# Cached decode attention, two blocks on one core: block B's output projection summed in four PSUM columns and stored element by element from two queues, instead of transposed to rows first

## The chip, the core and the metric

The kernel runs on one core of a Trainium2 chip. The metric is the device time of one execution, in microseconds (us). Before the change the median of three runs is 824.31 us (824.25 to 824.35).

## What is computed

Two independent blocks, A and B, each decode one token (one query row `x` of 512 values) with 32 heads of 128 and a cache of 16384 keys and values per head. A attends to all 16384 positions, B to the last 4096 only.

```python
q = (x @ wq).reshape(B, Sq, Hq, Dh).transpose(0, 2, 1, 3)
scores = einsum("bhqd,bhkd->bhqk", q, k) * (Dh ** -0.5)    # B: k, v = the last 4096 positions
p = softmax(scores, axis=-1)
o = einsum("bhqk,bhkd->bhqd", p, v)
y = o.transpose(0, 2, 1, 3).reshape(B, Sq, Hq * Dh) @ wo   # wo: 4096 x 512
out = concatenate([y_A, y_B], axis=-1)                     # 1 x 1 x 1024, bf16
```

The change lies in the last product, for B: 512 output values, each a sum over the 4096 rows of `wo`.

## The kernel before, in words

Keys, values and weights are bf16 and come from HBM in transfers of 2 or 4 MB (the pieces at the end are smaller), almost all issued by SyncE (SP). The work is cut into 20 units: B's first, then A's sixteen (two heads each), then B's other three. For each unit VectorE (DVE) multiplies a key tile by the broadcast query (L437) and adds up over the head's width in a tree of additions (L449, L456). ScalarE (ACT) makes the exponentials (L516), TensorE (PE) multiplies them by the values (L564). Two key tiles and one value tile are in turn refilled as they come free.

Every operation is recorded with what it reads and writes. The recorder works out the semaphore waits, and each engine's instructions run in the order in which they were recorded. A transfer is issued by the queue of the engine it was recorded on: SP's (`L.dma_start`) or ACT's (`S.dma_start`).

The end of the program, where the change lies, is in this order:

- SP issues the last half tile of B's values and then B's `wo` in five pieces of 16, 8, 4, 3 and 1 rows per partition (`wo_pieces`, L765). After these SP has nothing left but the store of B's result and the wait at the end.
- PE projects A's result as one row (`project_out_rows`, L640); ACT copies it and stores it with its own queue (L646).
- The last unit's scores, softmax and products with the values follow (L604, each half scaled by DVE at L611). `permute_o` (L620 to L632) then puts B's 4096 attention outputs into `OpB`, 128 partitions by 32.
- `project_out_columns` does B's projection. For each piece of `wo`, as it lands, PE does 4 matmuls per row of the piece (L656): a 128x128 block of `wo` is the weight, one column of `OpB` the moving side, so that 128 of the 512 outputs come as one PSUM column. Each piece has four columns of its own in the bank `OC2`, so there are 20 in all.
- DVE adds the five pieces (L665), into `cols`, 128 partitions by 4, f32. PE transposes it into 4 rows of 128 (L669). DVE casts these to bf16 (L671). SP stores the rows, 4 of 256 bytes (L672).
- SP waits for both stores (the semaphores `outA` and `outB`), and the program's closing barrier follows.

PE's program is cut at the marked operations in `parts`; the first piece's matmuls of the projection are the last mark. The cut stays at the same operation in both kernels.

Of the kernel before, what the change touches and what calls it, by code (L numbers as in the profile page):

```python
# [10 lines left out]
F32 = mybir.dt.float32  # L11
BF16 = mybir.dt.bfloat16
P = 128
ACT = mybir.ActivationFunctionType
ALU = mybir.AluOpType
AX = mybir.AxisListType

HQ, DH = 32, 128
# [209 lines left out]
def kernel(  # L228
# [19 lines left out]
    DN = A_wo.shape[1]  # L248
# [7 lines left out]
    def sb(name, shape, dtype):  # L256
        return pool.tile(shape, dtype, tag=name, name=name)

    def pst(name):
        return psum.tile([P, 512], F32, tag=name, name=name)  # L260
# [6 lines left out]
    identf = sb("identf", [P, P], F32)  # L267
# [10 lines left out]
    p_t = sb("p", [P, 2 * CH], BF16)  # L278
# [2 lines left out]
    pm_t = sb("pm", [P, 2 * CH * 4], BF16)  # L281
    r_t = sb("r", [P, 8], F32)
    osb = sb("osb", [P, 512], F32)
    cols = sb("cols", [P, 4], F32)
    sm = pst("sm")
    oc_t = pst("oc")
    TP = [pst(f"tp{i}") for i in range(2)]
    OC2 = pst("oc2")
# [16 lines left out]
    st = _Stream(tc)  # L305
    V, T_, S, G, L = nc.vector, nc.tensor, nc.scalar, nc.gpsimd, nc.sync
# [339 lines left out]
        st.op("ACT", lambda: S.dma_start(out=out[0, 0:1, 0:DN], in_=row), r=["osb"], w=["outA"], dma="outA")  # L646

    def project_out_columns(s, key, pieces):
        nf, npc = DN // P, len(pieces)
        ps = OC2[:, 0 : npc * nf].rearrange("p (k c) -> p k c", k=npc)  # L650
        r0 = 0
        for k, n in enumerate(pieces):
            def mms(k=k, n=n, r0=r0):
                for c in range(nf):
                    for r in range(r0, r0 + n):
                        x = T_.matmul(  # L656
                            ps[:, k, c : c + 1], lhsT=s.wo_t[:, r, c * P : (c + 1) * P], rhs=s.Op[:, r : r + 1],
                            start=(r == r0), stop=(r == r0 + n - 1),
                        )
                return x  # L660

            st.op("PE", mms, r=["Op" + s.n, f"{key}.{k}"], w=["oc2"])
            r0 += n
        first = st.ops["PE"][-npc]
        st.op("DVE", lambda: V.tensor_reduce(  # L665
            out=cols[:, :], in_=ps.rearrange("p k c -> p c k"), axis=AX.X, op=ALU.add
        ), r=["oc2"], w=["cols"])
        pr = TP[0][0:nf, 0:P]
        st.op("PE", lambda: T_.transpose(pr, cols[:, :], identf[:, :]), r=["cols", "identf"], w=["tp0"])  # L669
        rows = p_t[0:nf, 0:P]  # L670
        st.op("DVE", lambda: V.tensor_copy(rows, pr), r=["tp0"], w=["p.0", "p.1"])  # L671
        st.op("SP", lambda: L.dma_start(out=out[0, 0, DN : 2 * DN].rearrange("(c f) -> c f", c=nf), in_=rows),  # L672
              r=["p.0"], w=["outB"], dma="outB")
        return [first]

    wo_pieces = (16, 8, 4, 3, 1)
# [3 lines left out]
    for s in (B, A):  # L680
        s.x_row = flat(KS[1][0:1, :, :])[:, x0 : x0 + D]
        for a, b in x_pieces:
            st.op("ACT", lambda s=s, a=a, b=b: S.dma_start(out=s.x_row[:, a:b], in_=s.x[0, 0:1, a:b]),
                  w=[f"x{s.n}.{a}"], dma=f"x{s.n}{a}")
# [7 lines left out]
        out=identf[:, :], in_=identf[:, :], compare_op=ALU.not_equal, fill=1.0, base=0,  # L692
# [7 lines left out]
    for s in (B, A):  # L700
# [9 lines left out]
          w=["k10", "k11", *(f"x{n}.{a}" for n in "AB" for a, _ in x_pieces)] + [f"k10.{j}" for j in range(4)], dma="K10")  # L710

    parts = []
    for T, un in enumerate(units):
# [5 lines left out]
        if un.last:  # L719
            W, wk = KS[NT % 2], f"k{NT % 2}"  # L720
            s = A
# [41 lines left out]
    r0 = 0  # L763
    for i, n in enumerate(wo_pieces):
        st.op("SP", lambda r0=r0, n=n: L.dma_start(out=B.wo_t[:, r0 : r0 + n, :], in_=src[:, r0 : r0 + n, :]),  # L765
              r=["v1"], w=[f"wo.{i}"], dma=f"woB{i}")
# [12 lines left out]
    parts.append(st.ops["PE"][-1])  # L779
    mark = permute_o(B)  # L780
    parts += project_out_columns(B, "wo", wo_pieces)
    st.op("SP", lambda: None, r=["outA", "outB"], w=["end"])
    with tc.tile_critical(no_gpsimd_drain=True):
        st.finish(mark, parts)

# [29 lines left out]
```

## Time and profile before

| | us |
|---|---|
| median of the 3 runs | 824.31 |
| the profiled execution's own time | 824.25 |
| its span, from the first to the last instruction | 822.5 |
| DVE busy | 750.4 (91% of the span) |
| PE busy | 197.9 (24%) |
| ACT busy | 60.0 (7%) |
| last matmul of B's projection ends | 818.92 |
| SP issues the store of B's result | 819.89 |

The profiled execution's time is 1.8 us above its span: that part lies ahead of the first or behind the last instruction. The span is in microseconds from the first instruction. In the profile's lines "L656" is line 656 of the kernel, "out<-in" names the tiles written and read, "SPq" and "ACTq" are the instructions with which SP and ACT issue transfers, and a bracket at the end of a line gives the idle time ahead of it and who ended it. The core has 16 DMA engines, and a DMA packet is one run of bytes that one of them moves.

### The profile page before, as it was taken

What the parts mean: (1) busy time and instruction counts of PE and PEld (TensorE: products, weight loads), DVE (VectorE), ACT (ScalarE), POOL (GpSimd) and SP (SyncE); (2) the same over time, 40 slices, a digit from 0 to 9 for tenths busy, and PEclk for the clock granted to TensorE, in tenths of its full rate; (3) what the DMA queues carried; (4) which work ended last, traced back from release to release, by engine and by line L of the source; (5) the groups of instructions that cost most, each with busy time, mean ns of one, the idle gap of its engine ahead of it and who ended that gap; (6) DMA issues with size and microseconds to landing.
All of it is one profiled execution on the core that took longest, in us unless ns stands there. A gap on an engine that the chain in (4) does not pass through costs nothing. (4 is left out here: it accounts for less than half of the span.)

```text
span 822.5 us, 5105 instructions
## 1 busy us (share of the span) xinstructions
PE 197.9 (24%) x1985; PEld 99.0 (12%) x1985; DVE 750.4 (91%) x258; ACT 60.0 (7%) x168; POOL 0.7 (0%) x6
## 2 busy tenths in 40 slices
PE   3401212203030303030303212030303030303176
PEld 1100101101010101010101101010101010101035
DVE  2999899999999999999999999999999999999960
ACT  0101000001010100000000001010100000010111
POOL 0000000000000000000000000000000000000000
PEclk9765656565565655565655565555656555655575
DMA  9999999999999999999999999999999999999997
GB/s 383 433 433 433 457 412 450 418 447 421 444 424 441 427 437 430 437 430 437 430 437 430 437 430 437 430 437 430 437 430 437 430 422 445 422 433 431 432 432 298
DMA packets 8094, 352.44 MB, mean 429 GB/s; under 512 B 915, under 2 KB 1046, under 8 KB 1302
## 3 DMA queue, kind: packets, MB, share of 16 engines
q1 hardware_dynamic: 8072, 352.33, 99.2%
q8 instruction: 6, 0.10, 0.0%
q14 instruction: 2, 0.02, 0.0%
q10 hardware_dynamic: 14, 0.00, 0.0%
HBM read 352.32 MB, written 0.00 MB: 428 GB/s over the span
## 5 line engine op out<-in xcount | busy, mean ns | idle before, releaser
L449 DVE TENSOR_TENSOR k<-k 128x16384 bf16<-128x16384 bf16 (+3 forms) x84 | 333.3, 3968 | 2.2
L437 DVE TENSOR_TENSOR k<-k,qA 128x16384 bf16<-128x16384 bf16 x32 | 277.8, 8682 | 21.2 <-DVEq L122 21.1
L564 PE MATMUL oA<-v,pm 128*8 128x512 bf16 x1024 | 89.4, 525 | 111.0 <-PEq L122 111.0
L437 DVE TENSOR_TENSOR k<-k,qB 128x16384 bf16<-128x16384 bf16 x8 | 69.4, 8679 | 1.0 <-DVEq L122 1.0
L471 PE MATMUL sm<-identf,m 128*1 128x128 f32 x24 | 8.1, 369 | 207.8 <-PEq L122 207.8
L493 PE MATMUL sm<-one_f,Mr 1*128 1x1 f32 x48 | 12.4, 335 | 188.8 <-PEq L122 188.8
L564 PEld LDWEIGHTS oA<-v,pm 128*8 128x8 bf16 x1024 | 30.1, 110 | 163.7 <-issue 155.3
L456 DVE TENSOR_REDUCE sc<-k 128x256 f32<-128x2048 bf16 (+1 forms) x21 | 45.9, 2185 | 0.7
L493 PEld LDWEIGHTS sm<-one_f,Mr 1*128 1x128 f32 x48 | 11.2, 300 | 195.1 <-issue 195.1
L512 ACT ACTIVATE bias<-sm 128x1 f32<-128x1 f32 (+1 forms) x20 | 3.4, 171 | 412.0 <-ACTq L122 412.0
L471 PEld LDWEIGHTS sm<-identf,m 128*1 128x1 f32 x24 | 1.7, 80 | 209.7 <-issue 209.7
L576 ACT ACTIVATE osb<-oA,r 128x512 f32<-128x512 f32 x16 | 11.0, 687 | 214.1 <-ACTq L122 214.1
L564 PE MATMUL oB<-v,pm 128*16 128x512 bf16 x192 | 17.6, 546 | 23.1 <-PEq L122 23.1
L586 PE MATMUL oc<-selA,osb 128*128 128x2 f32 x128 | 16.4, 250 | 15.6 <-PEq L122 15.6
L586 PEld LDWEIGHTS oc<-selA,osb 128*128 128x128 f32 x128 | 15.5, 191 | 23.2 <-issue 23.2
L544 PE MATMUL sm<-cs,rowsA 128*128 128x1 f32 x32 | 8.9, 348 | 32.3 <-PEq L122 32.3
L502 ACT ACTIVATE pm<-p,maskA 128x256 bf16<-128x256 bf16 x32 | 14.5, 500 | 0.5
L544 PEld LDWEIGHTS sm<-cs,rowsA 128*128 128x128 f32 x32 | 8.0, 311 | 33.2 <-issue 33.2
L419 PE MATMUL tp<-v,osb 128*128 128x512 bf16 x32 | 9.1, 454 | 10.6 <-DMA v<-in_A_wq_dram 10.6
L516 ACT ACTIVATE p<-sc,bias 128x256 bf16<-128x256 f32 (+1 forms) x24 | 11.3, 470 | 0.6
L488 DVE TENSOR_REDUCE M<-sm 1x2 f32<-1x128 f32 (+1 forms) x20 | 6.0, 298 | 5.8 <-DVEq L122 5.8
L465 DVE TENSOR_REDUCE m<-sc 128x1 f32<-128x256 f32 (+1 forms) x20 | 8.4, 420 | 2.8
(73 smaller groups left out, 108.0 us busy)
## 6 DMA issues: line engine op xcount, KB each, us to landing
k<-in_B_k_cache_dram SPq DMA_DIRECT2D x8, 4096.0 KB, 35.9
v<-in_B_v_cache_dram SPq DMA_DIRECT2D x7, 4096.0 KB, 29.3
v<-in_B_wq_dram SPq DMA_DIRECT2D x1, 4096.0 KB, 12.2
v<-in_A_wq_dram SPq DMA_DIRECT2D x1, 4096.0 KB, 30.5
k<-in_A_wo_dram SPq DMA_DIRECT2D x1, 4096.0 KB, 33.5
k<-in_B_v_cache_dram SPq DMA_DIRECT2D x1, 4096.0 KB, 42.9
v<-in_B_wo_dram SPq DMA_DIRECT2D x1, 2048.0 KB, 25.1
v<-in_B_wo_dram SPq DMA_DIRECT2D x1, 1024.0 KB, 27.0
```

What stands on the lines that cost most here:

```text
L419: x = T_.matmul(out_ap, lhsT=s.xb[:, j, c, :], rhs=wq[:, c, j, g : g + 4, :], start=(k == 0), stop=(k == n - 1),)
L437: return V.tensor_tensor(out=k, in0=k, in1=s.q[:, bass.ds(i, 1), :].broadcast_to([P, CH, DH]), op=ALU.mult)
L449: st.op("DVE", lambda it=None, w=w: V.tensor_tensor(out=k[:, :, 0:w], in0=k[:, :, 0:w], in1=k[:, :, w : 2 * w], op=ALU.add), r=keys, w=keys)
L456: st.op("DVE", lambda it=None: V.tensor_reduce(out=sc[:, l0:l1], in_=un.K[:, l0:l1, 0:8], axis=AX.X, op=ALU.add), r=[f"k{un.k}{u}" for u i ...
L471: i = T_.transpose(sm[0:1, v * P : (v + 1) * P], m_t[:, v : v + 1], identf[:, :])
L493: i = T_.matmul(sm[:, 256 + v : 257 + v], lhsT=Mr[:, v * P : (v + 1) * P], rhs=one_f[:, :], start=True, stop=True,)
L502: return S.activation(out=out, in_=in_, func=ACT.Copy, scale=mask)
L516: st.op("ACT", lambda it=None, v=v: S.activation(out=p_t[:, v * n : (v + 1) * n], in_=sc[:, v * n : (v + 1) * n], func=ACT.Exp, scale=inv, ...
L544: i = T_.matmul(sm[v * w : (v + 1) * w, 264:265], lhsT=s.rows[:, :, :, :].rearrange("p r a b -> p (r a b)"), rhs=cs[:, v : v + 1], start=T ...
L564: x = T_.matmul(s.o[r0 : r0 + un.rows, :], lhsT=un.pm[:, l, :, :].rearrange("p a b -> p (a b)"), rhs=VS[:, 4 * l : 4 * l + 4, :], start=(i ...
L576: st.op("ACT", lambda it=None: S.activation(out=osb[:, :], in_=s.o[:, :], func=ACT.Copy, scale=r_t[:, 0:1]), r=["o" + s.n, "r"], w=["osb"] ...
L586: x = T_.matmul(oc_t[:, 0:w], lhsT=osb[:, j * P : (j + 1) * P], rhs=sel[:, j, :], start=(j == 0), stop=(j == 3),)
```

## The change

`project_out_columns` is rewritten. All five pieces add into the same four PSUM columns: only the first matmul of all has `start`, only the last has `stop`. DVE copies the four columns as bf16 into `cols` (now 128 x 4, bf16). The transpose on PE and the second cast on DVE are gone. The result is stored straight from `cols`. In `cols`, partition f holds outputs f, 128+f, 256+f and 384+f, so neighbours in a partition are 256 bytes apart in the output and every 2-byte element is a run of its own: 128 x 2 elements in a store by SP and 128 x 2 in one by ACT. SP's wait at the end is for three semaphores in place of two. On every other line the instructions of each engine and their order are the same in both kernels.

```diff
-    cols = sb("cols", [P, 4], F32)
+    cols = sb("cols", [P, DN // P], BF16)
...
     def project_out_columns(s, key, pieces):
-        nf, npc = DN // P, len(pieces)
-        ps = OC2[:, 0 : npc * nf].rearrange("p (k c) -> p k c", k=npc)
+        nf = DN // P
+        ps = OC2[:, 0:nf]
         r0 = 0
         for k, n in enumerate(pieces):
-            def mms(k=k, n=n, r0=r0):
+            def mms(r0=r0, n=n):
                 for c in range(nf):
                     for r in range(r0, r0 + n):
                         x = T_.matmul(
-                            ps[:, k, c : c + 1], lhsT=s.wo_t[:, r, c * P : (c + 1) * P], rhs=s.Op[:, r : r + 1],
-                            start=(r == r0), stop=(r == r0 + n - 1),
+                            ps[:, c : c + 1], lhsT=s.wo_t[:, r, c * P : (c + 1) * P], rhs=s.Op[:, r : r + 1],
+                            start=(r == 0 and c == 0), stop=(r == HQ - 1 and c == nf - 1),
                         )
                 return x
 
             st.op("PE", mms, r=["Op" + s.n, f"{key}.{k}"], w=["oc2"])
             r0 += n
-        first = st.ops["PE"][-npc]
-        st.op("DVE", lambda: V.tensor_reduce(
-            out=cols[:, :], in_=ps.rearrange("p k c -> p c k"), axis=AX.X, op=ALU.add
-        ), r=["oc2"], w=["cols"])
-        pr = TP[0][0:nf, 0:P]
-        st.op("PE", lambda: T_.transpose(pr, cols[:, :], identf[:, :]), r=["cols", "identf"], w=["tp0"])
-        rows = p_t[0:nf, 0:P]
-        st.op("DVE", lambda: V.tensor_copy(rows, pr), r=["tp0"], w=["p.0", "p.1"])
-        st.op("SP", lambda: L.dma_start(out=out[0, 0, DN : 2 * DN].rearrange("(c f) -> c f", c=nf), in_=rows),
-              r=["p.0"], w=["outB"], dma="outB")
+        first = st.ops["PE"][-len(pieces)]
+        st.op("DVE", lambda: V.tensor_copy(cols[:, :], ps), r=["oc2"], w=["cols"])
+        half = nf // 2
+        for eng, e, key, c0 in (("SP", L, "outB0", 0), ("ACT", S, "outB1", half)):
+            to = out[0, 0, DN + c0 * P : DN + (c0 + half) * P].rearrange("(c f) -> f c", c=half)
+            st.op(eng, lambda e=e, to=to, c0=c0: e.dma_start(out=to, in_=cols[:, c0 : c0 + half]),
+                  r=["cols"], w=[key], dma=key)
         return [first]
...
-    st.op("SP", lambda: None, r=["outA", "outB"], w=["end"])
+    st.op("SP", lambda: None, r=["outA", "outB0", "outB1"], w=["end"])
```

## The prediction

> **What bounds the kernel now.** I read the first page for the span, then the chain of work that ended last, in order of time, then the timeline of the last 5 us, then SP's own waits, and last the view of DMA traffic in short windows. The page says that the kernel streams its caches at one rate throughout, with VectorE nearly full beside it:
>
> ```profile
> PE 197.9 (24%) x1985; PEld 99.0 (12%) x1985; DVE 750.4 (91%) x258; ACT 60.0 (7%) x168; POOL 0.7 (0%) x6
> ...
> DMA  9999999999999999999999999999999999999997
> ```
>
> The DMA row is at nine tenths or more in 39 of 40 slices; the change touches neither the streams nor DVE's work on them. It can act only behind the last load. The chain shows where that is:
>
> ```profile
> 790.02 28.25 DMA v<-in_B_wo_dram
> ...
> 818.31 0.61 PE oc L656 x16
> ...
> 818.95 0.19 DVE cols L665
> ...
> 819.18 0.39 PE tp L669
> ...
> 819.59 0.28 DVE p L671
> ```
>
> The last piece of B's `wo` lands at 818.27, PE's last 16 matmuls end at 818.92, and then a reduction, a transpose and a cast run one after another, with nothing beside them. The timeline gives the store that follows, and SP's waits give how long SP then stands:
>
> ```profile
> 819.89 0.35 SPq L672 DMA_DIRECT2D out_dram<-p  x1
> ```
>
> ```profile
> SPq L672 <- DVE p L671: 29.0, 1, 29.0
> ...
> SPq L124 <- DMA out_dram<-p: 0.8, 1, 0.8
> ```
>
> SP waits 29.0 us for the cast, issues from 819.89 to 820.24, and waits 0.8 us for the store, until about 821.08. From there to the end of the span (822.5) is the closing barrier, 1.4 us, the same in both kernels. So what is at stake is 818.92 to 821.08, 2.16 us of 824.25: 0.97 us of work ahead of the store and 1.19 us of store. A measurement of this kernel can tell about 0.2%, 1.65 us, from no change. The program's own time, 824.25, is 0.06 below the median of the runs, 824.31; I add the sum to 824.25 and give the result for the runs, since 0.06 is smaller than any doubt below.
>
> **What is removed.** The matmuls stay: 128 at L656 in the same order and the same five pieces, writing other columns; nothing in their rows (163 to 187 ns each) hangs on the column, so 0. The reduction becomes a copy of the same PSUM bank, 128x4 bf16 from 128x4 f32. The kernel has exactly that form at its start:
>
> ```profile
> 9.81 0.16 DVE L399 CAST xTB<-tp 128x4 bf16<-128x4 f32 x1 [6.35 <-PE tp L392]
> ```
>
> So the copy begins at 818.95 and ends at 819.11. The stores can issue 0.02 later (the cast of before ended at 819.87, its store issued at 819.89), at 819.13. Against 819.89 that is **-0.76 us**, all of it on the path. It is also all that the change can win: the transpose, its two hand-overs and the cast. What is late next is the store itself.
>
> **What is added: 512 single elements.** Before, 4 runs of 256 bytes. Now 256 runs of 2 bytes on SP's queue and 256 on ACT's. The trace has no run of 2 bytes, so each stage of the store is bounded by rows.
>
> *Issue.* The rows are in the lists of the two lines that issue loads and of the one that issues `wo`:
>
> ```profile
> L335 SPq DMA_DIRECT2D v<-in_A_v_cache_dram x16: 327/328/334, 88.8 to 671.7; - x16
> ...
> L335 SPq DMA_DIRECT2D k<-in_B_k_cache_dram x8: 535/576/643, 1.4 to 718.8; - x8
> ```
>
> ```profile
> L765 SPq DMA_DIRECT2D v<-in_B_wo_dram x5: 432/432/592, 788.4 to 790.5; - x5
> ```
>
> With 128 rows an issue takes 0.33 to 0.64 us, and 0.43 for `wo`; the store of before took 0.35 with 4. I take 0.43: **+0.08** (from -0.02 to +0.29). ACT's issue runs beside SP's: ACT has been idle since 813.74 (L632), and behind the store it has only the barrier; behind SP's store is only the wait at the end. At the kernel's start ACT and SP issued at the same moment, and ACT's issue took 0.53 where its others took 0.21 to 0.38. So a collision of two issues is worth at most 0.32; I take 0.
>
> *From issue to the packets.* The store of before, in the DMA view of 820.6 to 820.8 (slices of 5 ns):
>
> ```profile
> DMA  0000000000000010112101001001000000000000
> ...
> DMA packets 8, 0.00 MB, mean 5 GB/s; under 512 B 8, under 2 KB 8, under 8 KB 8
> ...
> q1 hardware_dynamic: 8, 0.00, 3.0%
> ```
>
> Its first packet moves at 820.67, 0.43 after the issue ended, the last at 820.74. They are four runs of 256 bytes and four 4-byte semaphore writes: 3.0% of 16 engines' 0.2 us is 96 ns for 8, and in the packet records 15 ns for a run and 9 ns for a semaphore write. The only transfer with 128 rows that meets idle DMA engines is the first load: issued 0.96 to 1.38, and in the view of 1.9 to 2.7 its engines start between 2.00 and 2.66:
>
> ```profile
> DMA  0000999900999000009000000090000090900900
> ```
>
> That is 0.62 to 1.28 after the issue, +0.13 to +0.79 against the 0.49 of the old store's last packet. It reads HBM and is the kernel's first, so it is a high bound for a store; the low bound is 0. I take **+0.45**, the middle of the load's two ends.
>
> *The elements.* If they are dealt evenly, 512 over 16 engines are 32 each, and 2 semaphore writes. The nearest rows are the 15 ns of the smallest data packet written to HBM, and 9 ns, which is a 4-byte write. At 15 ns: 32 x 15 + 2 x 9 = 0.50 us, less the 0.02 that an engine had before: **+0.48** (+0.28 at 9 ns). The upper end is the time from the last packet to its landing, 820.74 to about 821.07, 0.33 us: paid by each element in turn, it is 32 x 0.33 = 10.6 us. The ends are far apart; the packet rows are nearer, since writes of before were sent within 15 ns of each other on one engine without waiting for a landing (run, then semaphore write). The landing of the last write itself, 0.33, stays.
>
> A rule bears on this size. The Trainium skill (VectorE: DVE Perf Modes, "The three transpose paths") says that a plain strided copy used as a transpose is 19 times slower than the transposing DMA, which takes 1309 ns for 128x128: as an estimate, 24.9 us for 16384 elements on 16 engines, 24 ns for one. By it the elements would add 0.77 and not 0.48, and the time would be about 824.9; no run here shows such a copy yet.
>
> *The end.* SP's wait is for one semaphore more; its branch with a wait took 33 ns (L335): **+0.03**.
>
> **The sum:** -0.76 + 0.08 + 0.45 + 0.48 + 0.03 = **+0.28**, so 824.25 + 0.28 = 824.5, and with the 0.06 to the median 824.6. With every low bound: -0.76 - 0.02 + 0 + 0.28 + 0 = -0.50, 823.8.
>
> **The rivals.**
>
> *A 2-byte write holds its engine (slower).* In place: between the first and the last packet of the two stores. All but the elements adds up to -0.20, so the change is slower by 1.65 us once the 34 packets cost 1.85 us more, about 57 ns an element. That is a sixth of the 0.33 us to a landing: it decides when an engine has fewer than six element writes on the way at once, or when writes to neighbouring addresses queue at the memory (512 elements fall into 1 KB of output). Three at once: 32 x 0.11 = 3.5, less 0.20, +3.3: 827.6. One at a time: +10.4, 834.7. [...] Against it: the 256-byte and 4-byte packets of 15 and 9 ns. Chance 0.42. The Trainium skill (DMA: Bandwidth & Descriptors, "Specifications") has a rule of this kind: a transfer below 512 bytes is read, modified and written. The 256-byte runs of before are below that too and took 15 ns, so the trace does not show it as a price per run; for 2 bytes no run does yet.
>
> *The elements are as cheap as the semaphore writes and the engines start together (a gain, but a small one).* This is the -0.50 above, 823.8. It needs 9 ns an element and a start like that of 4 runs. It is inside the same band as the forecast, and I count it there: 0.10 of the 0.55.
>
> *Faster by over 1.65 us.* The whole stretch at stake is 2.16 us, and the store alone cannot be shorter than its landing and its issue, about 1.1. Only a shift elsewhere in the program, which no edit makes, could do it: 0.03.
>
> **How the numbers follow.** Forecast, no change within 0.2%: 0.55 (its own range 823.8 to 825.9). Slower by over 0.2%: 0.42. Faster by over 0.2%: 0.03. The range 823.8 to 828.5 takes in the forecast and the rival up to about 140 ns an element; I leave out some 0.13 above and 0.04 below.
>
> **What would show each step.** In the changed profile: a DVE copy of some 0.16 us at L667 right behind the last matmul, and two issues at L671 some 0.24 us after that matmul, side by side; an issue of 0.33 to 0.64 us; some 512 more packets under 512 bytes; and SP's wait for the stores in place of 0.8 us, near 1.8. A wait of 3 us or more is the slower rival, and the DMA view then tells whether the packets themselves are long or the landing is late. If the copy or the issue is not where I put it, the gain of 0.76 is wrong; if ACT's issue starts when SP's ends, the two queues share what I took to be separate.

## The result, and the profile after

The changed kernel takes 837.24 us (median of 4 runs, 836.72 to 837.6) against 824.33 for the kernel before (4 runs, 824.25 to 824.36): a ratio of 1.0156, 95% interval 1.0139 to 1.0174. It is 12.9 us slower, and lies above the predicted range of 823.8 to 828.5.

The profiled execution took 837.60 with a span of 835.8, against 824.25 and 822.5. On its page the last of the 40 slices is almost empty; one slice is 21 us:

```profile
DMA  9999999999999999999999999999999999999991
GB/s 381 463 411 452 415 436 446 414 440 449 415 434 449 421 433 439 423 442 430 430 445 423 430 452 423 430 445 420 439 430 430 430 439 420 436 433 432 427 422 41
DMA packets 8630, 352.44 MB, mean 422 GB/s; under 512 B 1451, under 2 KB 1582, under 8 KB 1838
```

The third line shows 536 more packets under 512 bytes than the 915 before: 512 single elements and 32 semaphore writes, where the old store had 8 packets. The chain in order of time, and the end of the timeline:

```profile
818.37 0.61 PE oc L658 x16
818.98 0.02 issue
819.00 0.16 DVE cols L667
```

```profile
819.00 0.16 DVE L667 CAST cols<-oc 128x4 bf16<-128x4 f32 x1 [6.45 <-PE oc L658]
819.19 0.41 SPq L671 DMA_DIRECT2D out_dram<-cols  x1
819.20 0.47 ACTq L671 DMA_DIRECT2D out_dram<-cols  x1
```

From the last matmul's end (818.98) to the issue is 0.21 us, where it was 0.97. Then no engine has anything to do until SP's wait is over. SP's waits say for what:

```profile
SPq L671 <- DVE cols L667: 28.6, 1, 28.6
...
SPq L124 <- DMA out_dram<-cols: 14.7, 1, 14.7
```

SP waits 14.7 us for the stores in place of 0.8. The DMA view of 820 to 821 (slices of 25 ns) shows when the packets moved, and the list of L671 when the stores landed, counted from the start of their issue. A landing is the moment at which the profile records the last of the store's 16 semaphore increments:

```profile
DMA  0000056999777787952000000000000000000000
...
DMA packets 544, 0.00 MB, mean 1 GB/s; under 512 B 544, under 2 KB 544, under 8 KB 544
```

```profile
L671 SPq DMA_DIRECT2D out_dram<-cols x1: 408/408/408, 819.2 to 819.2; - x1
L671 ACTq DMA_DIRECT2D out_dram<-cols x1: 475/475/475, 819.2 to 819.2; - x1
...
DMA to landing us min/median/max: 15.1/15.2/15.3
```

All 544 packets (512 elements and 32 semaphore writes) lie in one band from 820.11 to 820.49. Then the records show no packet, and the semaphore increments come from 828.44 to 834.46. The DMA engines had let go of the last element 14 us before the store was confirmed as written.

The spans' difference is 13.34 us. From the two traces: the last matmul 0.06 later, -0.76 to the issue, +0.06 for the longer SP issue, +14.03 from the issue's end to the last landing (0.83 before, 14.86 after), -0.05 behind it. That adds up to 13.34.

### The profile page after: what moved, and what is told of

It reads as the page before. It is cut to its first block, busy times and chain, and to the rows that moved or that the text cites. A ratio compares the mean times of both kernels' runs of the same rounds, so it can differ in the third digit from the quotient of the medians.

```text
span 835.8 us, 5103 instructions
## 1 busy us (share of the span) xinstructions
PE 198.8 (24%) x1984; PEld 99.4 (12%) x1984; DVE 749.9 (90%) x257; ACT 60.0 (7%) x168; POOL 0.7 (0%) x6
## 5 line engine op out<-in xcount | busy, mean ns | idle before, releaser
L564 PE MATMUL oA<-v,pm 128*8 128x512 bf16 x1024 | 91.7, 537 | 111.1 <-PEq L122 111.1
L419 PE MATMUL tp<-v,k 128*128 128x512 bf16 x32 | 9.9, 486 | 2.5 <-DMA v<-in_B_wq_dram 2.5
```

What stands on the lines that cost most here:

```text
L419: x = T_.matmul(out_ap, lhsT=s.xb[:, j, c, :], rhs=wq[:, c, j, g : g + 4, :], start=(k == 0), stop=(k == n - 1),)
L564: x = T_.matmul(s.o[r0 : r0 + un.rows, :], lhsT=un.pm[:, l, :, :].rearrange("p a b -> p (a b)"), rhs=VS[:, 4 * l : 4 * l + 4, :], start=(i ...
```

## The experiments

Three theories of the 14 us. M: the memory takes small writes to one region in turn, whatever their address. E: each DMA engine has one small write on the way at a time. L: writes into the same 64-byte stretch of the output go one after another, different stretches beside each other. The measure is the time from the stores' first packet to their last landing, in the trace's records: 0.40 us before, 14.35 after. Runs without an interval are single looks, and the changed kernel's own four runs span 0.9 us, so differences of some tenths of a us between them say nothing. No run repeats the time from first packet to last landing. Each edit is against the changed kernel unless the text says otherwise; "..." marks lines left out.

### Half the elements

```diff
-        for eng, e, key, c0 in (("SP", L, "outB0", 0), ("ACT", S, "outB1", half)):
+        for eng, e, key, c0 in (("SP", L, "outB0", 0),):
...
-    st.op("SP", lambda: None, r=["outA", "outB0", "outB1"], w=["end"])
+    st.op("SP", lambda: None, r=["outA", "outB0"], w=["end"])
```

> The changed kernel, but ACT's store is left out (outputs 256 to 511 of B are not written): 256 single elements instead of 512. In the changed kernel the 544 packets are over 0.4 us after the first, and the last landing comes 14.35 us after the first packet. Theory M (the memory takes the 512 small writes to the same 1 KB one after another, 14.35 / 512 = 28 ns each): 256 x 28 = 7.2 us from first packet to landing, time about 830.4. Theory E (each of the 16 DMA engines has one small write on the way at a time, 14.35 / 32 = 0.45 us each): 16 each, 7.2 us as well, about 830.4. Theory L (writes into one 64-byte stretch of the output go one after another, 32 in each, 0.45 us each, different stretches beside each other): still 32 per stretch, 14.3 us, about 837.5.

Measured: 838.09 us, 14.90 from the first packet to the last landing.

```profile
SPq L124 <- DMA out_dram<-cols: 15.4, 1, 15.4
```

Half the writes, half the writes per engine and one queue in place of two, and the wait is as long. M and E fall. What stayed the same is how densely the elements lie: 32 in each 64 bytes.

### The same elements, farther apart

Both stores, 2 x 256 elements, go into a scratch tensor with a gap between neighbours; B's half of the output is not written. G is the gap in elements.

```diff
+        apart = nc.dram_tensor("apart", (DN, G), BF16, kind="Internal").ap()
...
-            to = out[0, 0, DN + c0 * P : DN + (c0 + half) * P].rearrange("(c f) -> f c", c=half)
+            to = apart[c0 * P : (c0 + half) * P, 0].rearrange("(c f) -> f c", c=half)
```

> The changed kernel with the same two stores of 256 single elements each, but into a scratch tensor in HBM where neighbours lie 64 bytes apart (32 KB in all) instead of into the output (B's half of the output is not written). Theory L: no two elements in one stretch, so landing within 1 us of the packets, about 824. Theory E: unchanged, 14.3 us, about 837.5. Theory M: between, by how large the region is whose writes queue: unchanged if 32 KB counts as one, less if it is spread over several.

> As the run with 64 bytes between neighbours, with 512 bytes (256 KB in all). Theory E: unchanged, about 837.5. Theories L and M: landing within 1 us of the packets, about 824; if M's queue is one for all small writes, unchanged.

Measured: 824.35 us at 64 bytes, 824.00 at 512.

```profile
SPq L124 <- DMA apart<-cols: 1.4, 1, 1.4
```

That is SP's wait at 64 bytes; at 512 it is 1.2. The packets are as many and as short as in the changed kernel (7 to 9 ns each), from the same queues, and the 14 us are gone. E falls a second time, and L's forecast holds. That the destination is now a scratch tensor is not the reason: with 4 bytes between neighbours, below, the same kind of tensor takes 10.58 us. Then the price by the number of writes in a stretch:

> Theory L held: 256 elements took as long as 512, and 64 bytes between neighbours brought the time to 824.35. Open is how long a stretch is and how the price grows with the writes in it. Here the same 512 elements go to scratch, 32 bytes apart. Theory L with a price of (14.35 - 1.02) / 31 = 0.43 us for each further write into the same 64 bytes: 1.02 + 0.43 = 1.45 us from the first packet to the last landing, about 824.8. If the stretch is 32 bytes: as with 64 apart, 1.02 us, about 824.3.

> Neighbours 8 bytes apart in scratch: 8 writes in each 64 bytes. Theory L (0.43 us for each further write in a stretch): 1.02 + 7 x 0.43 = 4.0 us from the first packet to the last landing, about 827.3. Theory Q (the price grows faster than the number of writes in a stretch, or hangs on how many engines write into it; the stores of 8-byte runs, also 8 writes in 64 bytes but from 8 neighbouring partitions, took 1.92 us): about 2 us, about 825.3.

> Neighbours 4 bytes apart in scratch: 16 writes in each 64 bytes. Theory L: 1.02 + 15 x 0.43 = 7.5 us from the first packet to the last landing, about 830.8. Theory Q: about 4 to 5 us, about 828.

| gap, bytes | writes in 64 bytes | first packet to last landing, us | above the 64-byte gap, for each further write | time, us |
|---|---|---|---|---|
| 512 | 1 | 0.88 | | 824.00 |
| 64 | 1 | 1.03 | | 824.35 |
| 32 | 2 | 1.60 | 0.57 | 824.63 |
| 8 | 8 | 4.36 | 0.48 | 827.55 |
| 4 | 16 | 10.58 | 0.64 | 833.75 |
| 2 (the change) | 32 | 14.35 | 0.43 | 837.60 |

The lists of the store's line, for gaps of 8 and of 4 bytes:

```profile
DMA to landing us min/median/max: 4.3/4.8/5.3
```

```profile
DMA to landing us min/median/max: 11.2/11.3/11.5
```

Counted by 64 bytes, each further write costs 0.4 to 0.6 us. L's forecasts of 1.45 and 4.0 us for 32 and 8 bytes were near (1.60 and 4.36), and theory Q's (about 2, and 4 to 5) were too low. For 4 bytes L missed as well: 10.58 us where it gave 7.5, so the steps are not even. The 64 bytes are the unit in which this study counts, not a measured boundary: 32 bytes apart cost 0.57 more than 64, and 64 cost 0.15 more than 512, one look each. Counted by 128 bytes, and from the 512-byte gap on, the same rows give 0.15 to 0.31 for each further write, and nothing here rules that out.

### Other partitions into the same stretch

```diff
-                            ps[:, c : c + 1], lhsT=s.wo_t[:, r, c * P : (c + 1) * P], rhs=s.Op[:, r : r + 1],
+                            ps[:, c : c + 1], lhsT=s.wo_t[:, r, 2 * (c % 2) + c // 2 : DN : nf], rhs=s.Op[:, r : r + 1],
...
-            to = out[0, 0, DN + c0 * P : DN + (c0 + half) * P].rearrange("(c f) -> f c", c=half)
+            to = out[0, 0, DN : 2 * DN].rearrange("(f a b) -> b f a", a=half, b=half)[c0 // half]
```

> The changed kernel with the columns of wo dealt in another order: partition f holds outputs 4f, 4f+2, 4f+1 and 4f+3; SP stores the first two, ACT the others, still 512 runs of 2 bytes and 32 in each 64 bytes. But the 32 come from 8 neighbouring partitions instead of 32. Theory L by the number of writes alone: unchanged, 14.3 us from first packet to last landing, about 837.5. If what counts is that different engines write into the same stretch: far shorter, 2 to 4 us, about 826.

Measured: 836.95 us, 13.34 from packet to landing. The writers of a stretch are 8 neighbouring partitions instead of 32, and the price is about the same. In this kernel both queues write into every stretch, 16 elements each, and SP's waits divide in two:

```profile
SPq L124 <- DMA out_dram<-cols: 7.2, 1, 7.2
...
SPq L335 <- DMA out_dram<-cols: 6.8, 1, 6.8
```

```profile
DMA to landing us min/median/max: 7.8/11.2/14.6
```

SP's store lands 7.8 us after its issue, ACT's after 14.6: 16 writes into each stretch for the first, and 6.8 us more, 0.43 each, for the 16 of the second.

### Longer runs, and fewer of them

```diff
-                            ps[:, c : c + 1], lhsT=s.wo_t[:, r, c * P : (c + 1) * P], rhs=s.Op[:, r : r + 1],
+                            ps[:, c : c + 1], lhsT=s.wo_t[:, r, c : DN : nf], rhs=s.Op[:, r : r + 1],
...
-            st.op(eng, lambda e=e, to=to, c0=c0: e.dma_start(out=to, in_=cols[:, c0 : c0 + half]),
-                  r=["cols"], w=[key], dma=key)
+        st.op("SP", lambda: L.dma_start(out=out[0, 0, DN : 2 * DN].rearrange("(f c) -> f c", c=nf), in_=cols[:, :]),
+              r=["cols"], w=["outB"], dma="outB")
```

> The changed kernel with the columns of wo dealt so that partition f holds outputs 4f to 4f+3: one store by SP with 128 runs of 8 bytes. If the price is by the write (theory M): 128 x 28 ns = 3.6 us from first packet to landing, about 827. Theory L: 8 writes in each 64 bytes, 8 x 0.45 = 3.6, about 827. Theory E: 8 per engine, 3.6, about 827. If the price were by the byte it would stay near 14 us.

Measured: 825.41 us, 1.92 from packet to landing.

```profile
SPq L124 <- DMA out_dram<-cols: 2.4, 1, 2.4
```

That is half of what all three theories gave. So a run of 8 bytes is cheaper than the count of writes says, or 16 stretches queue less than the 64 of the 8-byte gap. (The 8 writes of a stretch came from 8 neighbouring partitions in both of these runs.) One column alone, 8 bytes apart, was to tell these apart (against the kernel with the 8-byte gap):

```diff
-        for eng, e, key, c0 in (("SP", L, "outB0", 0), ("ACT", S, "outB1", half)):
-            to = apart[c0 * P : (c0 + half) * P, 0].rearrange("(c f) -> f c", c=half)
+        for eng, e, key, c0 in (("SP", L, "outB0", 0),):
+            to = apart[0:P, 0:1]
...
-            st.op(eng, lambda e=e, to=to, c0=c0: e.dma_start(out=to, in_=cols[:, c0 : c0 + half]),
+            st.op(eng, lambda e=e, to=to, c0=c0: e.dma_start(out=to, in_=cols[:, 0:1]),
```

> One column only (128 of B's 512 outputs): SP stores 128 runs of 2 bytes into scratch, 8 bytes apart, the same 8 writes in each of 16 stretches of 64 bytes as the store of 8-byte runs (1.92 us from first packet to last landing), from the same partitions, but with 2 bytes in each instead of 8. With 512 such elements in 64 stretches it took 4.36 us. Theory S (the size of a run matters: a write of 2 bytes costs more than one of 8): about 4.4 us, about 827.5. Theory C (size does not matter below 64 bytes, the number of stretches that queue at once does): about 1.9 us, about 825.3.

Measured: 825.77 us, 2.59 from packet to landing.

```profile
SPq L124 <- DMA apart<-cols: 3.1, 1, 3.1
```

It lies between the two: 0.67 us above the 8-byte runs, 1.77 below 512 elements in 64 stretches. Neither S nor C alone gives that. It also goes against L as it was put: with 8 writes in each 64 bytes, L gives 4.0 us whatever the number of stretches, and the runs gave 4.36 for 64 stretches (two queues) and 2.59 for 16 (one queue). With 32 writes in each, 8 stretches had taken as long as 16. How size, stretches and queues share this stays open.

### One part alone, and two versions without single elements

Only the sum into four columns, with transpose, cast and the store of rows as before (against the kernel before):

```diff
-        ps = OC2[:, 0 : npc * nf].rearrange("p (k c) -> p k c", k=npc)
+        ps = OC2[:, 0:nf]
...
-                            ps[:, k, c : c + 1], lhsT=s.wo_t[:, r, c * P : (c + 1) * P], rhs=s.Op[:, r : r + 1],
-                            start=(r == r0), stop=(r == r0 + n - 1),
+                            ps[:, c : c + 1], lhsT=s.wo_t[:, r, c * P : (c + 1) * P], rhs=s.Op[:, r : r + 1],
+                            start=(r == 0 and c == 0), stop=(r == HQ - 1 and c == nf - 1),
...
-        st.op("DVE", lambda: V.tensor_reduce(
-            out=cols[:, :], in_=ps.rearrange("p k c -> p c k"), axis=AX.X, op=ALU.add
-        ), r=["oc2"], w=["cols"])
+        st.op("DVE", lambda: V.tensor_copy(cols[:, :], ps), r=["oc2"], w=["cols"])
```

> One part of the change alone, on the kernel before: all pieces of wo add into four columns and DVE copies them (f32) instead of adding five pieces; transpose, cast and the store of four rows stay as before. By every theory the loss comes from the store, so no change: the copy is 0.02 us shorter than the reduction (0.16 against 0.18), 824.3.

Measured: 824.36 us, ratio 1.0001 (0.9991 to 1.001). This part is worth nothing either way; the loss is the store's.

Rows straight from PE, in four quarters of the bank:

```diff
+                            OC2[32 * c : 32 * c + 32, 0:P], lhsT=s.Op[:, r : r + 1].broadcast_to([P, 32]),
+                            rhs=s.wo_t[:, r, c * P : (c + 1) * P], start=(r == 0), stop=(r == HQ - 1),
...
+        rows = p_t[:, 0:P]
+        st.op("DVE", lambda: V.tensor_copy(rows, OC2[:, 0:P]), r=["oc2"], w=["p.0", "p.1"])
+        st.op("SP", lambda: L.dma_start(
+            out=out[0, 0, DN : 2 * DN].rearrange("(c f) -> c f", c=nf),
+            in_=p_t[:, 0:P].rearrange("(c k) f -> c k f", c=nf)[:, 0, :]), r=["p.0"], w=["outB"], dma="outB")
```

> A version meant to win the change's 0.7 us without single elements: for each row and each of the four blocks of 128 outputs one matmul with the column of OpB (repeated to 32 columns) as weight and the block of wo as the moving side, into the four 32-partition quarters of one bank; the quarters hold the outputs as rows, so DVE copies 128x128 to bf16 once (0.2 to 0.28 us) and SP stores 4 rows of 256 bytes from partitions 0, 32, 64 and 96 as before. If matmuls into different quarters run beside each other, as the four of L564 do (92 ns each with 512 moving columns), the projection keeps pace with the loads, and the reduction, transpose and hand-overs (0.66 us) go: about 823.65. If they run one after another at about 0.11 us, 128 of them take 14 us from 813.9 on: about 833.

Measured: 824.24 us against 824.35, ratio 0.9999 (0.999 to 1.0008): no change. Its timeline shows why:

```profile
818.45 0.62 PE L655 MATMUL oc<-v,OpB 128*32 128x128 bf16 x16 [0.31 <-DMA v<-in_B_wo_dram]
819.19 0.29 DVE L665 CAST p<-oc 128x128 bf16<-128x128 f32 x1 [6.56 <-PE oc L655]
819.51 0.66 SPq L666 DMA_DIRECT2D out_dram<-p  x1
```

PE keeps pace (16 matmuls in 0.62 us, as before) and the issue starts 0.44 us after the last matmul instead of 0.97, but it takes 0.66 us where 4 rows from partitions 0 to 3 took 0.35. Over half of the gain goes there. Another 0.17 goes between the issue's end and the first packet (0.60 us for 0.43 before; SP's wait for the store is 1.0 for 0.8). The next run stores one row from one partition instead (again against the changed kernel).

```diff
+        for c, eng, copy in ((0, "DVE", V.tensor_copy), (1, "ACT", S.copy), (2, "DVE", V.tensor_copy), (3, "ACT", S.copy)):
+            st.op(eng, lambda c=c, copy=copy: copy(rowb[:, c * P : (c + 1) * P], OC2[32 * c : 32 * c + 1, 0:P]),
+                  r=["oc2"], w=[f"rowb.{c}"])
+        st.op("SP", lambda: L.dma_start(out=out[0, 0:1, DN : 2 * DN], in_=rowb),
+              r=[f"rowb.{c}" for c in range(nf)], w=["outB"], dma="outB")
```

> The version with four quarters again, whose tail was 0.6 us shorter but whose store took 0.66 us to issue where the store of before took 0.35. Here DVE and ACT copy two quarters each (1x128, bf16) side by side into one partition, and SP stores one row of 1024 bytes. If the longer issue came with the partitions 32 apart, it goes back to 0.23 to 0.35 (ACT's one-row store of A took 0.23). The copies are 2 x 0.28 at most one behind the other on each engine. From the last matmul to the end of the issue: 0.02 + 0.45 to 0.56 + 0.03 + 0.35 = 0.85 to 0.96 us, against 1.32 before: about 0.4 us less, 823.95, a ratio of 0.9995. If any copy out of a quarter is slow, no gain, 824.3.

Measured: 823.99 us against 824.47, ratio 0.9994 (0.9985 to 1.0003).

```profile
819.09 0.54 ACT L665 CAST Mr<-oc 1x128 bf16<-1x128 f32 x2 [5.24 <-PE oc L655]
819.09 0.59 DVE L665 CAST Mr<-oc 1x128 bf16<-1x128 f32 x2 [6.50 <-PE oc L655]
819.71 0.33 SPq L667 DMA_DIRECT2D out_dram<-Mr  x1
```

The issue is back at 0.33, and from the last matmul (819.03) to its end is 1.01 us, where it was 1.32. That is a little above the 0.85 to 0.96 expected: the copies took 0.54 and 0.59 us. It has the lowest median of the versions that write the whole result, but the interval reaches 1: the gain is seen in the timeline and not settled by the times.

## Why the prediction was wrong, step by step

- **Removed work, -0.76:** right. The copy took 0.16, and matmul to issue shrank from 0.97 to 0.21.
- **Issue, +0.08:** right (0.41 for 0.43), and SP and ACT issued side by side. **Issue to packets, +0.45:** too much; the first packet came 0.51 after the issue's end, 0.08 later than before.
- **The elements, +0.48:** as time on the DMA engines this was too much; the packets took 7 to 9 ns and all were through 0.38 us after the first. Together these two terms were +0.93, and the traces give +0.40: the last packet started 0.89 us after the issue's end, and 0.49 before.
- The Trainium skill's factor for a strided copy (VectorE: DVE Perf Modes, "The three transpose paths"), 24 ns an element by my estimate, was too much for the sending as well, and the 824.9 us that it gave was far below the measured time. The page gives the factor for a large innermost stride at the destination, a condition that the prediction left out.
- **The end, +0.03:** nothing of it is seen; from the last landing to the end of the span it is 1.35 us, and 1.40 before.
- **"The landing of the last write itself, 0.33, stays":** this step failed. From the last packet to the last landing it was 13.97 us, so a term that the sum put at no change was +13.64. I had argued for the cheap end from packets that left one engine 15 ns apart. Such rows show how fast an engine sends. They say nothing about how fast the other side takes the writes in, and the store is over only when the last is confirmed. The row for that was there, 0.33 us, but it was of four runs of 256 bytes, not of single elements side by side.
- **What stays of the forecast:** with the same elements 64 bytes apart, the kernel took 824.35 us beside 824.40 for the kernel before. That is near the 824.6 of the forecast. So the terms ahead of the landing were sound enough, though the start and the elements were put 0.5 us too high together.
- **The slower rival** (0.42) had the right side and, in its second half, the place ("when writes to neighbouring addresses queue at the memory"). But it was priced by engine, 32 writes of 0.33 us. What decides is how densely the writes lie, here 32 in each 64 bytes, and not 32 per engine: half the elements, 16 per engine, took as long, and 64 bytes apart they took 1.03 us with 32 per engine. The price was 0.43 us, so the time also lay above that rival's worst, 834.7.
- **The Trainium skill's rule** (DMA: Bandwidth & Descriptors, "Specifications") that transfers below 512 bytes are read, modified and written may be what happens inside a stretch, but no run shows that. What the runs show is narrower: 512 writes of 2 bytes, each in a stretch of its own, landed within 1.03 us of their first packet, so being short is not by itself what costs 14 us.

That the 14 us pass after the last packet, and that they hang on how densely the elements lie in the destination, is shown. The exact law is not: the size of the stretch is open, and at 8 writes in 64 bytes the number of stretches or queues counted too. Whether the time arises in the memory itself or on the way to it was not tried.

## What to carry to other kernels

The time that a packet keeps its DMA engine and the time until a store has landed are two numbers; for a store at the end of a kernel only the second counts. Before a result is stored in single elements, count how many of them fall into the same 64 bytes: with 512 elements each further one cost here about half a us, and where two queues wrote into the same stretches, one store landed 6.8 us after the other. Work of 0.76 us that brings the result into runs of 256 bytes was cheap beside that.

## What the runs showed of the hardware that was not expected

- 512 single elements of 2 bytes, 64 bytes apart, landed 1.03 us after their first packet; the same elements side by side took 14.35.
- Issuing the store of 4 rows took 0.66 us from partitions 0, 32, 64 and 96, and 0.35 from partitions 0 to 3 (one profile each). The four packets behind it were as short, 15 to 16 ns, but the first came 0.60 us after the issue's end, and 0.43 in the other case.
- Four matmuls into four 32-partition quarters, 128 moving columns each, kept the pace of matmuls with one moving column: 16 in 0.62 us, against 0.61 before.
